# One load queue in order of need, an early ScalarE table load, and a new written-out order

## The chip, the cores and the metric

The kernel runs on one core of a Trainium2 chip. The core has five engines with a queue of instructions each: TensorE (PE, matmuls; its weight loads are listed as PEld), VectorE (DVE), ScalarE (ACT), GpSimd (POOL) and SyncE (SP, which here only issues transfers). Transfers run on the core's 16 DMA engines. They are issued from SP's or from ACT's queue, and an issue is an instruction of that queue like any other: what stands behind it waits for it. The metric is the device time of one execution in microseconds (us), as the median of several runs.

## What is computed

One transformer layer on x of 2048 tokens by 640 features, in bf16: linear attention with 32 heads of 20 features, and a feed-forward part with 1728 hidden features.

```python
def _A_ref(x, wqkv, w_phi, wo):
    qkv = (x @ wqkv).reshape(B, S, 3, H, Dh)           # q, k, v per head
    pq = einsum("bhsd,hdf->bhsf", q, w_phi)
    pk = einsum("bhsd,hdf->bhsf", k, w_phi)
    phi_q = concat([softmax(pq), softmax(-pq)], -1)
    phi_k = concat([softmax(pk), softmax(-pk)], -1)
    kv = einsum("bhsf,bhsd->bhfd", phi_k, v)
    z  = einsum("bhsf->bhf", phi_k)
    num = einsum("bhqf,bhfd->bhqd", phi_q, kv)
    den = einsum("bhqf,bhf->bhq", phi_q, z)[..., None] + 1e-6
    return (num / den) @ wo                            # heads joined again
def _B_ref(x, w1, w2):
    return silu(x @ w1) @ w2
h = x + _A_ref(layernorm(x), wqkv, w_phi, wo)
out = h + _B_ref(layernorm(h), w1, w2)
```

## The kernel before

The 2048 tokens are 16 tiles of 128, and 640 features are five chunks of 128. The whole program is a list of words, `ORDER`, read from left to right (lines 687 to 689). A word such as `kp.3` or `lx.1.2.a` calls `op_kp(3)` or `op_lx(1, 2, "a")`, and every engine's queue gets its instructions in the order of the words. Nothing is sorted later. So a word's place sets what it waits behind on its own engine. Semaphores between the engines are put in by the framework. A last letter names the engine or the queue: `a` is ACT, `v` DVE, `p` POOL, `s` SP. Ahead of the list stand eight filler matmuls (lines 685 and 686), and `wm` words add more; they multiply zeros and nobody reads them.

Stage 1 is the head. `lp` loads w_phi, `lk` chunks of the key weights into `wk`, `lv` those of the value weights into `wv`, `lx` tiles of x into `X`, `lo` the output weights. `wt.c` (line 301) transposes chunk c of `wk` with five matmuls, `wc.c` copies it from PSUM, `fk.c` (line 316) multiplies it with the block-diagonal w_phi that `ph` and `mk` build, and `fc.c` copies the result into `Wfk`, the key weights folded with w_phi. All five chunks are needed by every `kp`. `lq.c` loads a chunk of the query weights transposed, into `wk`'s space, once all `wt` have read it; `gk` and `gc` fold it in the same way.

Stage 2 does the keys and values. For tile t, `st` takes the statistics of the first layer norm on DVE, `rs` and `rm` finish them on POOL, `xn` normalises on DVE or ACT. Four tiles are transposed by PE (`xt`, copied by `xc`), twelve by a transposing transfer on SP (`xd`). `vp` and `kp` (line 344) are the two projections, ten matmuls each, `vc` copies the values, `ke` takes the two exponentials on ACT, `kr` sums and inverts them on DVE, `ka` scales them on POOL (`kb` half a tile on DVE), and `cc` (line 404) accumulates the key-value product, which `km` masks at the end of the stage.

Stage 3 does the queries and the attention's output. `qp.g.i` (line 424) projects the queries of four tiles for a part of the heads, and `qe` takes the exponentials. `dp` (line 458) is the product with the key-value matrix, `dw` and `dr` divide on DVE, `do` writes the two halves of a tile on DVE or POOL, `td` transposes it by a transfer, `op` (line 520) multiplies by the output weights, and `oa` adds the residual. `sq` (ACT), `sa` and `sr` (POOL) take the second layer norm's statistics, `hn` normalises and `hd` transposes it by a transfer.

Stage 4 is the feed-forward part, in groups of tiles (2, 4, 4, 4, 2): `up` (line 594 and 604), `ua` (Silu on ACT), `yp` and `yh` (line 640 and 655), `yo` adds the residual, `so` stores. `l1`, `l2` and `lh` load its weights. `ta` is a single exponential on one number, which makes ACT load the table that holds Exp. PSUM is four buffers of two banks, used by all products in turn.

Each transfer takes one of eight semaphores, in turn over both queues, so an issue waits for the eighth transfer before it.

Of the kernel before, what the change touches and what calls it, by code (L numbers as in the profile page):

```python
# [30 lines left out]
xn.4.v vp.0 ke.3 st.6 xd.4 xn.5.v kp.0 xc.1.a rs.6.2 st.8 lq.2 rm.6 st.11 kp.1 mc xn.6.a lq.1 xn.7.v
vc.0.a st.9 vp.1 xd.5 ke.0 st.15 kp.4 xd.6 vc.1.a st.10 ke.1 lq.4 gk.3 st.13 vp.4 rs.8.4 ke.4 xd.7
st.14 vp.5 rm.11 gc.3.a mo st.12 vc.4.a gk.1 kr.0 vc.5.a vp.6 rs.12.4 xn.11.a gc.1.a kp.7 xd.11 rm.8
rm.10 xn.13.v ka.0.p xn.10.a kr.1 kp.6 lq.0 vc.6.a ke.7 l1.2.s kr.4 kp.5 ka.1.p ke.6 kp.11 xn.8.a
xn.9.v xn.14.v xd.9 rm.15 kr.2 vp.7 rm.12 ke.11 ka.4.p xd.10 cc.1 vc.7.a kr.3 cc.0 ke.5 xd.13 vp.11
ka.2.p xn.12.a vp.9 kr.7 xn.15.a xd.12 ka.3.p kp.10 vc.9.a xd.8 kr.5 vc.11.a gk.4 ke.10 kp.13 xd.15
ka.7.p gc.4.a kr.10 xd.14 vp.10 kp.12 ka.5.p vc.10.a kr.6 cc.7 cc.2 ke.12 cc.4 ka.10.p cc.3 vp.14
ke.13 kr.12 kp.14 ka.6.p vc.14.a kr.13 gk.0 vp.13 gc.0.a ka.12.p kr.11 cc.10 vc.13.a cc.5 ke.14 kp.9
ka.13.p kp.8 ke.9 gk.2 kr.9 vp.8 ka.11.h gc.2.a kp.15 vc.8.a kr.14 ka.9.p qp.0.0 ke.15 ke.8 ka.14.p
qp.0.2 qe.0.0 kr.8 qp.0.1 qe.0.2 kr.15 ka.8.p vp.12 qe.0.1 kb.11 vp.15 ka.15.p vc.12.v cc.13 vc.15.v  # L40
# [6 lines left out]
dw.9.v sq.5 td.3 ua.0.3 sr.5 l2.8.13.s dp.6 do.4.0.v ua.0.1 up.0.2 dr.9 td.4 dw.6.v l2.0.4.s op.3
ua.0.2 dp.8 oa.3 op.10 dw.8.v sa.3 sq.3 sa.2 up.0.0 sr.3 dr.6 dr.8 do.6.1.p oa.10 op.4 ua.0.0 sr.2
hn.5 do.8.0.v do.8.1.p dp.7 oa.4 yp.1.1 td.8 hn.2 sa.4 sq.4 hn.3 do.9.1.p dw.7.v hd.3 sr.4 yp.1.0
hd.5 do.6.0.p do.9.0.v yh.0.0 td.6 hn.4 dp.11 yp.0.0 dw.11.v hd.2 yp.0.1 td.9 yo.1 hd.4 op.8 op.6  # L50
oa.8 dr.11 sa.8 yo.0 op.9 dr.7 so.0 oa.6 up.1.4 oa.9 sq.6 sa.9 sq.8 do.11.0.p up.1.0 ua.1.4 sa.6
sr.8 sa.10 dp.15 ua.1.0 up.1.1 dw.15.v sq.9 sr.9 up.1.3 ua.1.1 do.11.1.v sr.6 dr.15 do.15.1.v
do.7.0.p do.15.0.v do.7.1.v up.1.6 ua.1.3 hn.9 td.7 td.11 dp.13 ua.1.6 up.1.5 dw.13.v td.15 dp.12
ua.1.5 op.11 dw.12.v op.7 oa.11 up.1.2 oa.7 dr.13 dr.12 dp.14 ua.1.2 op.15 dw.14.v yp.2.0 oa.15 hn.6
yh.1.1 sa.15 sq.15 yh.1.0 dr.14 hd.6 do.12.0.v sa.11 yp.3.1 sq.10 do.13.0.v do.14.0.p sq.7 do.14.1.p
yp.2.1 sr.10 sa.7 hn.10 do.13.1.v sr.7 yp.4.1 yo.2 hn.8 sr.15 so.2 hn.7 td.13 do.12.1.v yp.5.0 hd.8
yp.3.0 td.14 op.13 hd.7 hd.9 yp.4.0 so.1 td.12 yp.5.1 yo.4 yo.3 so.4 hd.10 op.14 yo.5 up.2.3 oa.14
oa.13 sa.14 sa.13 up.2.1 up.2.2 up.2.5 ua.2.2 ua.2.3 ua.2.1 up.2.0 up.2.6 ua.2.0 sq.14 up.2.4 ua.2.6
ua.2.5 op.12 ua.2.4 sq.11 yp.7.1 oa.12 sr.11 sq.12 hn.11 yh.2.0 sq.13 yh.2.1 yp.9.1 sr.13 sr.14
yp.8.1 sa.12 hn.14 hn.15 sr.12 hd.14 yp.9.0 hn.12 hd.15 yp.8.0 yo.9 so.3 hd.11 yp.6.0 so.5 yo.8  # L60
hn.13 so.8 yp.6.1 so.9 hd.12 yp.7.0 yo.6 so.6 hd.13 up.4.2 yo.7 so.7 up.4.3 up.4.1 ua.4.3 ua.4.2
# [655 lines left out]
```

## Time and profile before

| | |
|---|---|
| median of 3 runs | 247.22 us (246.47 to 247.43) |
| the profiled execution | 246.91 us |
| its span | 244.9 us |
| PE busy | 235.9 us, 2148 matmuls |
| DVE, ACT, POOL busy | 135.2, 108.8, 87.3 us |
| mean granted clock | 0.993 |
| bytes moved | 20.60 MB |

The span runs from the first to the last recorded instruction. The profiled execution's own time has 2.0 us around it. Times in what follows are counted from the span's start. In a timeline's row, the first number is the start and the second the time from the first instruction's start to the last one's end; "xN" is the number of instructions, and the brackets give the idle time of the engine before them and what ended it. "ACTq" and "SPq" are the issuing of transfers in ACT's and SP's queue. The granted clock is a share of TensorE's full speed.

### The profile page before, as it was taken

Reading aid. Unit: us, or ns where it says so; the run is one execution under the profiler, and the core shown is the slowest. Engines: PE = TensorE matmul, PEld = TensorE weight load, DVE = VectorE, ACT = ScalarE, POOL = GpSimd, SP = SyncE. Lnnn points to the kernel's source line nnn. Section 1 sums busy time; section 2 is a strip of 40 time slices with the busy share of each in tenths; the row PEclk is TensorE's granted clock in tenths of the full one; section 3 lists DMA queues with packets and bytes.
Section 4 is the critical chain, followed back from the end, with each engine's and each line's share of the span. In section 5 each row is a group of like instructions: output and inputs, shape, how many; then the busy total and the mean of one; then the engine's idle time right before and its main releaser. Section 6 shows DMA issues by size and latency. Waiting matters only on the chain.

```text
span 244.9 us, 5196 instructions
## 1 busy us (share of the span) xinstructions
PE 235.9 (96%) x2148; PEld 152.2 (62%) x2162; DVE 135.2 (55%) x259; ACT 108.8 (44%) x158; POOL 87.3 (36%) x165
## 2 busy tenths in 40 slices
...
GB/s 191 357 306 66 133 60 198 102 12 0 3 3 0 29 195 173 182 173 116 121 95 3 54 29 27 60 117 95 0 3 28 174 97 0 0 3 0 0 87 76
DMA packets 42968, 20.60 MB, mean 84 GB/s; under 512 B 34368, under 2 KB 42560, under 8 KB 42944
## 3 DMA queue, kind: packets, MB, share of 16 engines
...
q8 instruction: 17, 0.28, 0.5%
q14 instruction: 7, 0.06, 0.1%
...
## 4 chain that ended last, share of the span: by engine, by line
PE 83%; DMA 6%; DVE 4%; SPq 2%; issue 2%; ACT 1%; POOL 1%; DVEq 0%; POOLq 0%
PE mm L594 23%; PE mm L640 20%; PE mm L344 18%; PE mm L520 6%; PE mm L424 5%; PE mm L404 3%; PE mm L458 2%; DMA HnT<-hn 2%; PE mm L316 2%; DMA X<-in_A_x_dram 2%; SPq L579 1%; DMA ot<-o 1%; PE mm L604 1%; DMA phr<-in_A_w_phi_dram 1%; DVE u L474 1%
## 5 line engine op out<-in xcount | busy, mean ns | idle before, releaser
L594 PE MATMUL mm<-HnT,w 128*128 128x512 bf16 (+1 forms) x317 | 58.0, 336 | 1.2 <-DMA HnT<-hn 0.7
L640 PE MATMUL mm<-w,shT 128*128 128x320 bf16 (+2 forms) x415 | 58.1, 299 | 0.1
L616 ACT ACTIVATE shT<-mm 128x1024 bf16<-128x1024 f32 (+2 forms) x29 | 27.0, 965 | 60.2 <-PE mm L594 43.9
L640 PEld LDWEIGHTS <-shT 128*128 128x128 bf16 x416 | 39.8, 98 | 17.3 <-issue 1.1
L594 PEld LDWEIGHTS <-w 128*128 128x128 bf16 x325 | 31.2, 98 | 24.7 <-DMA HnT<-hn 1.0
L663 DVE TENSOR_TENSOR ob<-mm,X 128x640 bf16<-128x640 f32 x15 | 12.1, 818 | 49.6 <-PE mm L640 42.5
L344 PEld LDWEIGHTS <-XnT 128*128 128x128 bf16 x320 | 30.7, 98 | 11.6
L382 POOL TENSOR_TENSOR Ek<-Ek,Sk 128x1280 bf16<-128x1280 bf16 (+1 forms) x16 | 36.7, 2322 | 2.3 <-DVE Sk L377 2.3
L374 DVE TENSOR_REDUCE Sk<-Ek 128x64 f32<-128x1280 bf16 x16 | 23.2, 1449 | 5.2 <-ACT Ek L366 5.2
L434 ACT ACTIVATE EqT<-mm 128x1024 bf16<-128x1024 f32 (+1 forms) x24 | 19.6, 888 | 10.9 <-PE mm L424 10.7
L520 PE MATMUL mm<-wo,ot 128*128 128x320 bf16 x160 | 23.9, 299 | 0.3 <-DMA ot<-o 0.2
L344 PE MATMUL mm<-wv,XnT 128*128 128x320 bf16 x160 | 23.9, 299 | 0.0
L344 PE MATMUL mm<-Wfk,XnT 128*128 128x320 bf16 x160 | 23.5, 299 | 0.0
L424 PE MATMUL mm<-XnT,Wfq 128*128 128x512 bf16 x95 | 22.8, 380 | 0.6 <-ACT EqT L434 0.3
L529 DVE SCALAR_TENSOR_TENSOR X<-mm,X 128x640 bf16<-128x640 f32 x16 | 12.8, 813 | 17.5 <-PE mm L520 17.5
L366 ACT ACTIVATE Ek<-mm 128x640 bf16<-128x640 f32 x32 | 20.5, 715 | 3.6 <-PE mm L344 2.3
L537 ACT ACTIVATE sq<-X 128x640 bf16<-128x640 bf16 x16 | 11.8, 735 | 21.4 <-DVE X L529 18.6
L520 PEld LDWEIGHTS <-ot 128*128 128x128 bf16 x160 | 15.2, 98 | 7.0 <-DMA ot<-o 0.5
L542 POOL TENSOR_SCALAR HM<-HST 128x1 f32<-128x1 f32 x16 | 3.7, 234 | 43.9 <-DVE X L529 43.9
L493 POOL TENSOR_TENSOR o<-u,rd 128x320 bf16<-128x320 f32 x18 | 13.1, 744 | 14.0 <-PE mm L424 9.7
L424 PEld LDWEIGHTS <-Wfq 128*128 128x128 bf16 x100 | 9.2, 98 | 11.0 <-issue 0.6
L474 DVE TENSOR_TENSOR u<-mm,w 128x672 f32<-128x672 f32 x16 | 13.7, 858 | 1.4 <-DVE w L472 0.3
...
## 6 DMA issues: line engine op xcount, KB each, us to landing
...
```

The costliest lines, as they stand in the source:

```text
L344: nc.tensor.matmul(ps[:, half, 0:320], tok(XnT[t // GT], t)[:, c, :], W[:, c, half * 320 : (half + 1) * 320], start=(c == 0), stop=(c == C ...
L366: nc.scalar.activation(Ek[:, s, :].rearrange("p (a n) -> p a n", a=2), tl["kp", t][:, :, 0:320], AF.Exp, scale=1.0 - 2.0 * s,)
L374: nc.vector.tensor_reduce(Sk[:], tl["ek", t][:].rearrange("p s (h f) -> p (s h) f", f=DH), axis=AX.X, op=ALU.add,)
L382: eng.tensor_tensor(Ek3, Ek3, tl["sk", t][:, lo:hi].unsqueeze(2).to_broadcast([P, hi - lo, DH]), op=ALU.mult,)
L424: nc.tensor.matmul(ps[:, k, :], Wfq[:, c, r * P : (r + 1) * P], XnT[g][:, c, :], start=(c == 0), stop=(c == C - 1),)
L434: nc.scalar.activation(E[:, s, rs[0] : rs[-1] + 1, :], tl["qp", g, i][:, 0 : len(rs), :], AF.Exp, scale=1.0 - 2.0 * s,)
L474: nc.vector.tensor_tensor(u[:], A[1][:, :, :, 0:21], w[:].unsqueeze(3).to_broadcast([P, 2, 16, 21]), op=ALU.mult,)
L493: (nc.vector if eng == "v" else nc.gpsimd).tensor_tensor(tl["o", t][:, a * 320 : (a + 1) * 320].rearrange("p (h f) -> p h f", f=DH), tl["u ...
L520: nc.tensor.matmul(ps[:, half, 0:320], tl["ot", t][:, c, :], wo[:, c, half * 320 : (half + 1) * 320], start=(c == 0), stop=(c == C - 1),)
L594: nc.tensor.matmul(ps[:, i * W : (i + 1) * W], w1[:, c, fc * P : (fc + 1) * P], HnT[g][:, c, 0:W], start=(c == 0), stop=(c == C - 1), skip ...
L616: nc.scalar.activation(sh[:, a:b], tl["up", g, k][:, 0 : b - a], AF.Silu)
L640: nc.tensor.matmul(ps, shT[g][:, fc * W + i * P : fc * W + (i + 1) * P], w2[:, fc, a:b], start=first and fc == 0, stop=last and fc == FC - ...
```

## The change

Only the list of words changes. At its head, all plain loads that stood on ACT's queue but w_phi's go to SP's (`lx.2.3.a` and `lx.3.4.s` become one `lx.2.4.s`, three `lv` become two), in another order: X 2:4, chunks 2, 0, 1 of `wk`, X 0, chunks 3 and 4, X 1, X 4:8, `wv`, and later X 8:12 and X 12:16. `lo` moves from the head to the middle. `ta` moves from near the end to ACT's second place. There are three `wm` words instead of six. The chunks are transposed in the order 2, 0, 1, 3, 4 instead of 1, 0, 4, 2, 3, and the folding follows; three `xt` stand ahead of the first projection, which is `kp.3` instead of `vp.2`.

After that the same operations come in another order throughout. Ten `xn` become fourteen on DVE, and ACT's six become two, with four `rm` less on POOL. Of the 32 halves of `do`, POOL gets 26 instead of 18. `l1`, `lh` and most `l2` words move from stage 3 into stage 2. `qp.1.2` comes before `km`, and `qp.3.2` and its `qe.3.2` come after the first group's `up` and `ua`.

```diff
 ORDER = """
-lp.a lk.1.2.s lx.2.3.a lk.0.1.s lk.4.5.a lk.3.4.s mk lk.2.3.a lx.3.4.s lx.0.1.a lv.0.2.s lv.2.4.a
-lv.4.5.s lx.1.2.a lx.4.8.s ph lo.s wt.1 st.2 wc.1.a wm.512 wm.512 wm.512 wt.0 lx.8.12.a rs.2 fk.1
-wc.0.v wt.4 fc.1.a wc.4.v wm.256 wt.2 fk.0 xn.2.v wc.2.a st.3 wm.512 xt.2 fc.0.a wt.3 fk.2 xc.2.a
-lq.3 wc.3.v fk.4 rs.3 fc.2.a wm.256 fk.3 vp.2 fc.4.a xn.3.v lx.12.16.s st.0 fc.3.a xt.3 st.1 kp.2
...
-cc.8 cc.11 cc.14 cc.9 cc.12 cc.6 cc.15 qp.1.0 km.1 close km.0 dp.1 qe.1.0 qp.1.1 dw.1.v dp.0 qe.1.1
-dr.1 qp.1.2 dw.0.v qe.1.2 qp.2.2 dr.0 do.1.1.v dp.2 qe.2.2 do.0.1.p qp.2.0 dw.2.v do.1.0.p do.0.0.p
-td.1 dp.5 td.0 qe.2.0 qp.2.1 dw.5.v lh.s l1.0.s dp.3 dr.2 qe.2.1 dr.5 op.1 dw.3.v do.5.1.p do.2.1.p
-op.0 do.5.0.p do.2.0.p oa.1 td.5 dp.10 oa.0 qp.3.2 td.2 dw.10.v sa.0 sq.0 qp.3.1 sa.1 l1.1.s sq.1
-sr.0 qe.3.2 sr.1 dr.10 hn.0 dp.4 qe.3.1 dr.3 hd.0 hn.1 qp.3.0 do.3.1.p dw.4.v hd.1 op.5 l2.4.8.s
-qe.3.0 dr.4 do.4.1.v op.2 oa.5 do.10.0.v sa.5 up.0.3 oa.2 do.10.1.p do.3.0.p dp.9 td.10 sq.2 up.0.1
...
-up.3.5 up.4.0 up.3.4 ua.4.0 ua.3.5 ta up.3.2 ua.4.1 up.3.6 ua.3.4 up.3.0 ua.3.6 ua.3.2 up.3.1 up.3.3
...
+lp.a lx.2.4.s ta lk.2.3.s lk.0.1.s mk lk.1.2.s lx.0.1.s lk.3.4.s lk.4.5.s lx.1.2.s st.3 lx.4.8.s
+wt.2 lv.3.5.s ph wt.0 lv.0.3.s wc.2.a wt.1 st.2 wc.0.a fk.2 wc.1.a st.0 wm.512 wt.3 rs.2.2 fc.2.a
+fk.1 wt.4 fc.1.a wc.3.v fk.0 rs.0 lq.1 wc.4.v wm.256 fk.3 fc.0.a xn.3.v fk.4 xn.2.v fc.3.a xt.3
+lx.8.12.s xn.0.v xt.2 fc.4.a xc.3.v lq.3 xt.0 st.6 wm.256 kp.3 xc.0.a xc.2.a lx.12.16.s st.7 lq.0
+kp.0 ke.3 st.1 rs.6.2 lq.4 kp.2 st.5 ke.0 rs.1 xn.6.v vp.3 st.4 ke.2 xd.6 xn.1.v rs.4.2 vp.2 st.11
+lq.2 vc.3.a mc st.9 xt.1 vp.0 xc.1.a st.10 vc.2.a gk.3 xn.5.v vc.0.a gk.0 xn.7.v vp.1 st.8 gc.0.a
+xd.7 xn.4.v rs.8.4 kp.1 kr.0 xd.5 vc.1.a gc.3.a gk.4 xd.4 vp.6 gc.4.a xn.10.v ka.0.p st.14 ke.1
+l1.1.s kp.6 lh.s st.13 vc.6.a st.15 kp.5 mo ke.6 st.12 gk.1 rm.8 gk.2 xn.9.v vp.4 rs.12.4 gc.2.a
...
+cc.11 cc.14 cc.13 cc.2 cc.10 vc.12.v cc.15 cc.8 cc.12 qp.1.0 km.1 close km.0 dp.1 qe.1.0 qp.1.1
+dw.1.v dp.0 qe.1.1 dr.1 qp.3.0 dw.0.v dp.3 qe.3.0 dr.0 qp.2.0 dw.3.v do.0.0.p do.0.1.p td.0 dp.5
+qe.2.0 dr.3 qp.2.1 do.3.1.v do.3.0.p dw.5.v do.1.1.p do.1.0.p op.0 td.1 qe.2.1 dr.5 do.5.1.p td.3
+dp.4 oa.0 do.5.0.p qp.2.2 dw.4.v sq.0 sa.0 td.5 op.1 sr.0 qe.2.2 hn.0 dp.2 dr.4 hd.0 op.3 oa.1
+do.4.0.p dw.2.v do.4.1.p sq.1 qp.3.1 sa.1 td.4 sr.1 hn.1 op.5 oa.3 qe.3.1 hd.1 dr.2 do.2.0.p op.4
+l2.0.4.s oa.5 do.2.1.v dp.10 td.2 up.0.2 dw.10.v up.0.3 oa.4 ua.0.2 dr.10 dp.9 ua.0.3 do.10.1.p sq.5
+up.0.1 dw.9.v sa.5 dp.6 ua.0.1 dr.9 up.0.0 dw.6.v do.9.1.p sq.3 sr.5 do.10.0.p op.2 hn.5 ua.0.0
+do.9.0.p dr.6 hd.5 sq.4 dp.8 oa.2 qp.3.2 td.10 dw.8.v sa.2 sq.2 yp.0.0 td.9 qe.3.2 sr.2 do.6.0.p
...
```

More of the change, by code (lines that the diff above doesn't have):

```diff
@@ L25 @@
 ORDER = """
-lp.a lk.1.2.s lx.2.3.a lk.0.1.s lk.4.5.a lk.3.4.s mk lk.2.3.a lx.3.4.s lx.0.1.a lv.0.2.s lv.2.4.a
-lv.4.5.s lx.1.2.a lx.4.8.s ph lo.s wt.1 st.2 wc.1.a wm.512 wm.512 wm.512 wt.0 lx.8.12.a rs.2 fk.1
-wc.0.v wt.4 fc.1.a wc.4.v wm.256 wt.2 fk.0 xn.2.v wc.2.a st.3 wm.512 xt.2 fc.0.a wt.3 fk.2 xc.2.a
-lq.3 wc.3.v fk.4 rs.3 fc.2.a wm.256 fk.3 vp.2 fc.4.a xn.3.v lx.12.16.s st.0 fc.3.a xt.3 st.1 kp.2
-rs.0 xc.3.a st.4 rs.1 vp.3 ke.2 xn.0.v st.5 xt.0 kp.3 xc.0.a xn.1.v rs.4.2 st.7 vc.2.a xt.1 vc.3.a
@@ L31 @@
[L31 to L40, printed above, removed]
@@ L46 @@
-qe.3.0 dr.4 do.4.1.v op.2 oa.5 do.10.0.v sa.5 up.0.3 oa.2 do.10.1.p do.3.0.p dp.9 td.10 sq.2 up.0.1
[L47 to L61, printed above, removed]
-up.3.5 up.4.0 up.3.4 ua.4.0 ua.3.5 ta up.3.2 ua.4.1 up.3.6 ua.3.4 up.3.0 ua.3.6 ua.3.2 up.3.1 up.3.3
-ua.3.1 ua.3.0 yp.15.1 ua.3.3 yh.4.0 yh.3.0 yp.12.1 yp.10.1 yp.15.0 yp.12.0 yo.15 yp.14.0 yp.14.1
@@ L64 @@
-yp.10.0 yo.14 yo.12 so.14 yh.3.1 yp.11.0 yo.10 so.10 yp.11.1 so.15 so.12 yq.13.0 yo.11 so.11 yq.13.1
-yz.13.0 yz.13.1 sz.13.0.a sz.13.1.s
+lp.a lx.2.4.s ta lk.2.3.s lk.0.1.s mk lk.1.2.s lx.0.1.s lk.3.4.s lk.4.5.s lx.1.2.s st.3 lx.4.8.s
+wt.2 lv.3.5.s ph wt.0 lv.0.3.s wc.2.a wt.1 st.2 wc.0.a fk.2 wc.1.a st.0 wm.512 wt.3 rs.2.2 fc.2.a
+fk.1 wt.4 fc.1.a wc.3.v fk.0 rs.0 lq.1 wc.4.v wm.256 fk.3 fc.0.a xn.3.v fk.4 xn.2.v fc.3.a xt.3
+lx.8.12.s xn.0.v xt.2 fc.4.a xc.3.v lq.3 xt.0 st.6 wm.256 kp.3 xc.0.a xc.2.a lx.12.16.s st.7 lq.0
@@ new lines @@
+kp.0 ke.3 st.1 rs.6.2 lq.4 kp.2 st.5 ke.0 rs.1 xn.6.v vp.3 st.4 ke.2 xd.6 xn.1.v rs.4.2 vp.2 st.11
+lq.2 vc.3.a mc st.9 xt.1 vp.0 xc.1.a st.10 vc.2.a gk.3 xn.5.v vc.0.a gk.0 xn.7.v vp.1 st.8 gc.0.a
+xd.7 xn.4.v rs.8.4 kp.1 kr.0 xd.5 vc.1.a gc.3.a gk.4 xd.4 vp.6 gc.4.a xn.10.v ka.0.p st.14 ke.1
+l1.1.s kp.6 lh.s st.13 vc.6.a st.15 kp.5 mo ke.6 st.12 gk.1 rm.8 gk.2 xn.9.v vp.4 rs.12.4 gc.2.a
+kr.6 xd.9 ke.5 vp.5 xd.10 xn.8.a xn.12.v ka.6.p xn.13.v kp.4 vc.5.a kr.3 xd.8 vc.4.a kp.7 ke.4 rm.11
+kr.5 ka.3.p vp.7 gc.1.a ke.7 qp.0.2 kr.4 xn.11.a kp.10 qe.0.2 xd.11 kr.7 ka.4.p vp.9 xd.12 kp.9
@@ new lines @@
+xn.14.v vc.9.a xn.15.v ka.7.p vc.7.a kr.2 xd.15 kp.11 l2.8.13.s xd.13 cc.4 ka.5.p cc.3 ke.10 cc.6
+l1.0.s cc.0 xd.14 cc.7 ke.9 kr.10 qp.0.0 l1.2.s ke.11 lo.s l2.4.8.s kr.9 ka.10.p kp.15 qe.0.0 kp.12
+kr.1 ke.15 ka.9.p qp.1.2 ke.12 kr.15 vp.8 ka.1.p vp.11 vc.8.a kr.11 qe.1.2 cc.5 ka.15.p cc.9 cc.1
+kr.12 kp.13 vc.11.a ka.11.p vp.10 ke.13 kp.14 vc.10.a kr.13 ka.12.h kp.8 ke.14 ka.2.p vp.14 ke.8
+kr.14 qp.0.1 vc.14.a kr.8 ka.14.p vp.13 kb.12 ka.13.p vp.15 vc.13.v vp.12 vc.15.a ka.8.p qe.0.1
+cc.11 cc.14 cc.13 cc.2 cc.10 vc.12.v cc.15 cc.8 cc.12 qp.1.0 km.1 close km.0 dp.1 qe.1.0 qp.1.1
@@ new lines @@
+do.9.0.p dr.6 hd.5 sq.4 dp.8 oa.2 qp.3.2 td.10 dw.8.v sa.2 sq.2 yp.0.0 td.9 qe.3.2 sr.2 do.6.0.p
+dr.8 yh.0.0 hn.2 sa.3 dp.7 yp.1.0 sr.3 dw.7.v do.6.1.p yp.1.1 sa.4 do.8.1.p do.8.0.v dr.7 sr.4 hn.3
+op.10 hd.3 yo.1 td.8 dp.11 oa.10 yp.0.1 dw.11.v sq.10 td.6 op.9 hd.2 hn.4 yo.0 op.8 hd.4 oa.9 op.6
+oa.8 sa.8 dp.13 oa.6 sa.9 up.1.5 dw.13.v sa.6 sq.6 do.7.0.p do.7.1.p up.1.1 ua.1.5 sr.6 td.7 dr.11
+dr.13 sq.8 do.11.1.p sq.9 do.11.0.p dp.15 up.1.2 td.11 dw.15.v sr.9 sr.8 up.1.3 sa.10 ua.1.2 ua.1.1
```

13 lines of the change are left out of this document (added).

## The prediction

> **What bounds the kernel now.** I read the page first, then PE's work and idle time by stage, then the timeline and the waits of the first 20 us, then the transfers.
>
> ```profile
> PE 235.9 (96%) x2148; PEld 152.2 (62%) x2162; DVE 135.2 (55%) x259; ACT 108.8 (44%) x158; POOL 87.3 (36%) x165
> PE 83%; DMA 6%; DVE 4%; SPq 2%; issue 2%; ACT 1%; POOL 1%; DVEq 0%; POOLq 0%
> ```
>
> TensorE is busy and carries the chain that ended last. Cut where the first projection begins (14.84 us, when its weights are loaded) and where the last matmul ends (241.86):
>
> ```profile
> 14.84:80.00 65.16, 64.96 (x777) 45.40 (x777) 54.91 (x94) 48.23 (x72) 47.53 (x51) 1.00 0.35 68
> 80.00:100.00 20.00, 19.46 (x188) 10.43 (x189) 18.43 (x39) 12.70 (x19) 8.41 (x19) 1.00 0.68 136
> 100.00:130.00 30.00, 29.10 (x304) 20.87 (x306) 22.07 (x49) 10.44 (x18) 11.98 (x34) 1.00 0.60 130
> 241.86:244.90 3.04, 0.00 (x0) 0.00 (x0) 0.29 (x1) 0.00 (x0) 0.00 (x0) 1.00 0.19 54
> sum 230.06, PE 224.94 PEld 145.26 DVE 129.09 ACT 103.27 POOL 83.79; mean PE 32.13 PEld 20.75 DVE 18.44 ACT 14.75 POOL 11.97
> ```
>
> The first number after the stretch is its length, the second PE's busy time. Over 227.02 us PE works 224.94 us and idles 2.1. A new order of the same work can save there at most these 2.1. The sum: 14.84 head + 224.94 work + 2.1 idle + 3.04 tail = 244.9, the span; the profiled execution took 246.91, 2.0 more. So the head is the place to win. In it:
>
> ```profile
> 7.22 0.33 ACTq L219 DMA_DIRECT2D X<-in_A_x_dram  x1
> 7.58 1.28 ACT L161 ACT_TABLE_LOAD   x1 [7.58 <-DMA X<-in_A_x_dram]
> 8.88 0.69 ACT L161 COPY wTk<-mm 128x640 bf16<-128x640 bf16 x1
> 9.62 0.49 PE L316 MATMUL mm<-phb,wTk 128*128 128x140 bf16 x6 [2.49 <-ACT wTk L161]
> 9.95 0.44 PE L301 MATMUL mm<-ident,wk 128*128 128x128 bf16 x5
> 14.89 1.52 PE L344 MATMUL mm<-wv,XnT 128*128 128x320 bf16 x10
> ```
>
> ScalarE stands in `lx.1.2.a`, an issue that must wait for an earlier transfer's semaphore, until 7.22, then loads its table, and only then copies the chunk whose transpose ended at 5.4. PE's queue is in order, so `fk.1` and all behind it wait 2.49 us, though the last piece of `wk` landed at 7.7 (issued 2.3, 5.4 to landing).
>
> ```profile
> 7.00:8.00 1.00, 0.13 (x2) 0.00 (x0) 0.49 (x1) 0.42 (x1) 0.00 (x0) 1.00 1.02 375
> 8.00:9.00 1.00, 0.00 (x0) 0.00 (x0) 0.00 (x0) 0.99 (x2) 0.00 (x0) 1.00 0.98 356
> 11.00:12.00 1.00, 1.00 (x8) 0.60 (x6) 1.00 (x3) 0.91 (x2) 0.00 (x0) 0.50 1.01 396
> 12.00:13.00 1.00, 0.94 (x10) 0.86 (x9) 0.28 (x2) 0.52 (x2) 0.52 (x2) 0.50 0.98 371
> ```
>
> The last three numbers are the granted clock, the DMA share and GB/s: the gap is paid twice, since quarter-microsecond windows show the clock at half from 10.35 to 13.76. DMA is full from 2 to 15 us.
>
> **The change, part by part.** *Landings.* All loads stand on one queue. From before's windows the bytes moved by 3, 4, ... 12 us are 0.25, 0.57, 0.80, 1.13, 1.46, 1.84, 2.19, 2.53, 2.88, 3.27 MB; a landing follows its last byte by about 0.8 (X 12:16: last bytes about 19.3, landed 20.1). In the new order X 2:4 lands at 3.9, `wk` 2, 0, 1 at 4.6, 5.2, 5.8, X 0 at 6.4, `wk` 3, 4 at 6.9, 7.3, X 1 at 7.8, X 4:8 at 9.6, `wv` at 10.6 and 12.0. Seven issues of 0.33 to 0.55 leave ACT; on SP eight of 0.43 end at 4.1, ahead of the bytes. The ninth transfer on must wait for the eighth before it, but over 1 MB is queued then: no gap. The last `wk` piece gains only 0.4 us.
>
> *ScalarE.* One issue (0.46), then the table, 1.28: ready at 2.6 instead of 8.86.
>
> *The head's chain*, with before's durations: transposes of a chunk 0.54 at half clock, 0.28 at full; `fk` 0.6 and 0.3; ACT copies 0.65; DVE statistics 1.1, mask product 1.0, copy 0.5, normalisation 0.42. The first eight fillers run at half clock (0.43 apart; the 128x512 matmul takes 0.22 later), and I take full clock from 6.9, one window of 3.41 (13.76 less 10.35) before 10.35: fillers were still 0.43 apart at 6.0, and `wt.4` at 10.1 took 0.28.
> PE: `wt.2` 4.63 to 5.17, `wt.0` to 5.75, `wt.1` to 6.35, `fk.2` to 6.9, filler, `wt.3` to 7.5, `fk.1`, `wt.4`, `fk.0` to 8.4.
> ACT: `wc.2`, `wc.0`, `wc.1` 5.3 to 7.2; `fc.2` to 7.9, `fc.1` to 8.6, `fc.0` to 9.25.
> DVE: `st.3` from 3.9, `ph` to 6.05, `st.2`, `st.0` to 8.2, `wc.3`, `wc.4` to 9.2, `xn.3`, `xn.2`, `xn.0` to 10.45, `xc.3` to 10.95.
> So `fk.3` 8.8 to 9.1, `fk.4` 9.3 to 9.6, `fc.4` 9.85 to 10.5, `xt.3`, `xt.2`, `xt.0` by 10.8, and `kp.3`, the first projection, at 11.1: DVE sets it. Two more transposes (0.56) are then done than at 14.84 before. Gain 14.84 - 11.1 + 0.56 = 4.3 us.
>
> *Fillers.* Before issues six after the first eight, after three; all fit in waits, so 0. Without that cover (PE never waiting) they would cost 0.4 at full clock.
>
> *What follows the first projection.* PE has 12 us of work up to `vp.6` (8 projections of 1.36, three `gk` of 0.32, a transpose), due at 23.2. `vp.3` (15.2) needs `wv` (12.0). `vp.6` needs `xd.6`, behind 4.9 MB on SP. At 0.35 MB/us for loads and 0.18 for the transposes among them (0.194 at 16 to 17) its bytes end near 19.6, landed by 20.6: slack 2.6. Its `xn.6` is ready at 15.7. `wo` (800 KB) no longer stands among the loads.
>
> *The normalising chain.* DVE and POOL must come forward with PE. DVE takes four `xn` of 0.41 from ACT (0.95 each), +1.6; POOL sheds four `rm` of 0.33. `kr.0` starts at about 22.4 (29.93 before), the last `kr` (2.0 each) ends near 61, the last `ka` (2.2 each) at 63, and its `cc` is due at about 69 (the last `cc` ends at 11.1 + 58.4 - 0.56 + 1.13 = 70.1, the 58.4 from 14.84 to 73.24 before). Before, the last `ka` ended at 72.15, some 0.6 ahead of its `cc`. So no new wait: 0.
>
> *To the first `up`.* After the last `cc`, PE had 25.9 us of work up to `up.0.3` and idled about 1.5; now it has 25.0 (`qp.1.2` has gone ahead, `qp.3.2` behind, one `op` comes in). Replaying the DVE chain (`dw` 2.4, `dr` 0.35, `oa` 0.85, `hn` 0.45) and the two halves of `do` on POOL (0.74 each), `hd.1` lands 25.9 after the last `cc`: about 1.1 idle, where before paid 1.5. Before's `hd.1` took 5.4 to land among w1 and w2 loads (2.6 where none run); those loads now go into 24 to 50 us. Eight more `do` halves lie on POOL (6.0 there, 3.4 less on DVE). At best all idle here goes (-1.1); at worst two tokens of the chain pay a second POOL half of 0.74 each (+1.5). I take 0 against before, as POOL is only 12 of 30 us busy at 100 to 130.
>
> *Table loads in the middle.* `qe.3.2` (Exp) now stands behind the first `ua` (Silu), so the compiled order has three loads there instead of one, and none at the end, where `ta` had two:
>
> ```profile
> 208.77 1.28 ACT L249 ACT_TABLE_LOAD   x1
> 210.27 1.28 ACT L616 ACT_TABLE_LOAD   x1
> ```
>
> PE lost 0.05 around those. In the middle ACT is busy 10.4 of 30 us; 2 x 1.28 hide, at worst 2.6 where `sq`, and so `hn`, stands behind them. I take 0, nearest to the row at 208.77. The Trainium skill's page "ScalarE: Activation LUTs" (What ACT_TABLE_LOAD costs) speaks against the move: it adds a drain of about 1.38 to each switch, 2.66 in all, so up to 5.3 here. Here the copy behind the load of 7.58 starts at 8.88, 1.30 after it, and so no drain shows.
>
> Sum: 11.1 + (224.94 - 0.56) + 2.1 + 3.04 = 240.6, and 2.0 around it: 242.6 against 246.91. The median shown (247.22) is 0.3 above the profiled run, so **242.9** as a median, 1.7% faster. A difference under 0.5% (1.2 us) is what a measurement of this kernel can't tell from none.
>
> **Rivals.** *The clock stays or goes low* (0.16). With fewer fillers the window up to 6.9 holds more transposes (1.6 us of 3.4, against 1.0). If the gate then opens only at 10.3, the head's chain becomes PE's: +0.7, 243.6. If the gaps between 6.9 and 10.3 (PE about 73% busy; 27% closed it before, 97% opened it) close it up to 13.8, the projections lose half of 3.41: +1.7, 244.6. The Trainium skill's "TensorE: Matmul & The Clock Gate" (Part 4: PE-mode transpose) says that transposes do not count as busy in the same way; by that the first of these times holds. The trace does not decide: the window before 6.9 opened the gate with 30% transposes.
>
> *The middle gets a new wait* (0.13): the switches and POOL's extra halves delay `sq`, `sr`, `hn`, and up.1 waits as up.0 did. Price 1.3 to 4: 244 to 247, say 245.5. For it: the only PE waits after 14 us lie at `up` and `op` behind such chains (0.7 and 0.2). Against: up.1 has a slack of about 1.7 by the same replay.
>
> *Slower* (0.12, of which 0.10 over the bound): one queue is too slow. `vp.6` waits for `xd.6`, which stands behind every load and four weight transposes, 5.1 MB in all. It gets as late as before's time plus 0.5% if it lands at 28.8 instead of 23.2 (a loss of 4.3 + 1.2), that is at a mean below 0.20 MB/us. For it: windows with transposes moved 194 to 213 GB/s (15 to 17 us). Against: SP's queue alone moved 371 and 355 GB/s at 96 to 97 and 100 to 101 us. At 0.19 the time is about 249.5.
>
> *The reordering buys nothing*: `wk` lands hardly sooner, so this part can be empty, and ACT's freedom alone still brings nearly all, since DVE's list sets 11.1. It is inside the forecast. *More* (0.04): no idle at `up.0` and a head of 10.3, 241.0 or less.
>
> **How the numbers follow.** Forecast 0.55 (241.0 to 243.9). 241.0 to 246.0 holds it, the clock and two thirds of the middle rival: 0.80. Faster by over 0.5% (below 246.0): 0.55 + 0.16 + 0.09 + 0.04 = 0.84; within: 0.06; slower: 0.10.
>
> **What would show it.** ACT's table load before 3 us and no wait of PE for `wTk` over 0.6; first projection at 10.3 to 12, `kp.3` behind DVE's `xc.3`; granted clock 1.00 from 7 us on, or half windows for the rival; PE idle from there to the last matmul about 2.1; `vp.6` without a wait at 23; `up.0.2` near 96.2 (100.66 before); table loads near 95 to 115. I am wrong if PE idles more than 3 us after the first projection, or that comes later than 12.5.

## The result, and the profile after

The changed kernel takes 243.74 us (median of four runs, 243.62 to 244.17), the kernel before 246.84 in the same comparison. The ratio is 0.9877 (0.9847 to 0.9907): 1.2% or 3.1 us faster, where 242.9 us and 1.7% were forecast. The profiled execution took 243.84 us with a span of 241.7, against 246.91 and 244.9. In a later comparison, together with the last four kernels below, the changed kernel came out at 0.9932 (0.9903 to 0.9961), so its gain is 2 to 3 us.

The page of the changed kernel, engines and then the chain that ended last:

```profile
PE 233.3 (97%) x2143; PEld 150.3 (62%) x2159; DVE 137.0 (57%) x255; ACT 105.8 (44%) x154; POOL 89.8 (37%) x167
...
PE 74%; DVE 15%; DMA 4%; POOL 3%; ACT 1%; issue 1%; POOLq 0%; ACTq 0%
```

TensorE is as busy as before, but it carries 74% of the chain instead of 83%, and DVE 15% instead of 4%. That is the first sign that something besides PE now sets a stretch. The head first, in the timeline of all engines and, for the last two rows, of PE:

```profile
1.28 1.28 ACT L249 ACT_TABLE_LOAD   x1 [1.28 <-PEq L701]
...
4.70 1.37 PE L301 MATMUL mm<-ident,wk 128*128 128x128 bf16 x15
...
5.19 1.88 ACT L161 COPY wTk<-mm 128x640 bf16<-128x640 bf16 x3 [2.41 <-PE mm L301]
...
10.29 4.24 PE L344 MATMUL mm<-Wfk,XnT 128*128 128x320 bf16 x30
14.37 2.88 PE L344 MATMUL mm<-wv,XnT 128*128 128x320 bf16 x20
```

ACT has its table at 2.6 us and copies the first chunk at 5.19 (8.88 before); the first projection starts at 10.29 (14.89). With the two transposes (0.56) that are now done ahead of it, the head gives 14.89 - 10.29 + 0.56 = 5.2 us. From there to the last matmul's end the kernel before took 241.86 - 14.89 = 227.0 us, 226.4 without those transposes. The changed one takes 238.7 - 10.29 = 228.4, so 2.0 are lost behind the head, and 5.2 - 2.0 = 3.2 is the whole difference of the spans. PE's waits behind the head say where:

```profile
PE mm L404 <- POOL Ek L382: 2.0, 3, 0.9
PE mm L316 <- DMA wk<-in_A_wqkv_dram: 0.8, 1, 0.8
PE mm L458 <- ACT EqT L434: 0.2, 1, 0.2
```

(The numbers are us in total, how often, and the longest.) `cc` waits three times, 2.0 us in all, for POOL's scaling `ka`, and `gk.0` waits 0.8 for a chunk of the query weights. These 2.8 are new. Some 0.8 of idle time elsewhere has gone, the stall at the first `up` above all, which leaves the 2.0. The same waits in PE's timeline:

```profile
19.99 0.23 PE L316 MATMUL mm<-phb,wk 128*128 128x140 bf16 x1 [0.76 <-DMA wk<-in_A_wqkv_dram]
...
41.95 1.72 PE L404 MATMUL mm<-Vp,Ek 128*64 128x84 bf16 x80 [0.43 <-POOL Ek L382]
44.35 0.57 PE L404 MATMUL mm<-Vp,Ek 128*64 128x84 bf16 x20 [0.68 <-POOL Ek L382]
...
55.60 0.57 PE L404 MATMUL mm<-Vp,Ek 128*64 128x84 bf16 x20 [0.90 <-POOL Ek L382]
```

POOL is not simply too slow: it stands and waits for DVE's sums, 1.9 us at a time (second and last row of the second fence below). So the question is what DVE does. DVE's timeline, then POOL's:

```profile
22.23 1.48 DVE L374 TENSOR_REDUCE Sk<-Ek 128x64 f32<-128x1280 bf16 x1
...
24.48 0.88 DVE L259 BATCH_NORM_STATS2 stats<-X 128x6 f32<-128x320 bf16 x2
...
28.50 0.39 DVE L276 TENSOR_SCALAR xn<-X,MV,RS 128x640 bf16<-128x640 bf16 x1
...
30.79 2.77 DVE L276 TENSOR_SCALAR xn<-X,MV,RS 128x640 bf16<-128x640 bf16 x2
33.48 1.47 DVE L374 TENSOR_REDUCE Sk<-Ek 128x64 f32<-128x1280 bf16 x1
...
41.25 3.23 DVE L276 TENSOR_SCALAR xn<-X,MV,RS 128x640 bf16<-128x640 bf16 x2
44.40 1.47 DVE L374 TENSOR_REDUCE Sk<-Ek 128x64 f32<-128x1280 bf16 x1
```

```profile
31.02 2.36 POOL L382 TENSOR_TENSOR Ek<-Ek,Sk 128x1280 bf16<-128x1280 bf16 x1 [0.91 <-ACT xn L281]
...
35.62 2.36 POOL L382 TENSOR_TENSOR Ek<-Ek,Sk 128x1280 bf16<-128x1280 bf16 x1 [1.88 <-DVE Sk L377]
39.55 7.15 POOL L382 TENSOR_TENSOR Ek<-Ek,Sk 128x1280 bf16<-128x1280 bf16 x3 [1.57 <-ACT Vp L161]
48.57 15.15 POOL L382 TENSOR_TENSOR Ek<-Ek,Sk 128x1280 bf16<-128x1280 bf16 x7 [1.87 <-DVE Sk L377]
```

A normalisation `xn` takes 0.39 us at 28.50, but two of them take 2.77 at 30.79 and 3.23 at 41.25, where POOL scales a tile. An `xn` that starts while a scaling runs ends 0.2 us after that scaling; one that starts before it is not held (0.35 us for the one at 30.79). All durations of `xn` on DVE, shortest, median and longest in ns, in the kernel before and in the changed one:

```profile
L276 DVE TENSOR_SCALAR xn<-X,MV,RS x10: 380/416/1271, 10.8 to 37.3; 128x640 bf16<-128x640 bf16 x10
```

```profile
L276 DVE TENSOR_SCALAR xn<-X,MV,RS x14: 347/418/2505, 8.6 to 42.0; 128x640 bf16<-128x640 bf16 x14
```

The four late ones should take 4 x 0.41 = 1.6 us and take 6.0, so 4.4 us of DVE are lost, and the sums (1.45) and all that stands behind them in DVE's queue come so much later. The sums themselves and the statistics run beside POOL at their usual durations. The row of before already held one such case, 1.271, which the median of 0.416 hid. The Trainium skill's page "SBUF — State Buffer" (SBUF: two separate sides) states a rule that fits: DVE, for some of its instructions, and GpSimd share a pair of ports, which the instruction that starts first holds for its whole length while the other engine is blocked. For `xn` against the scaling the trace agrees, 2.5 us in place of 0.39. That the ports are the reason is not shown here.

### The profile page after: what moved, and what is told of

Its sections match the earlier page's. It is cut to its first block, busy times and chain, and to the rows that moved or that the text cites. A ratio compares the mean times of both kernels' runs of the same rounds, so it can differ in the third digit from the quotient of the medians.

```text
span 241.7 us, 5181 instructions
## 1 busy us (share of the span) xinstructions
PE 233.3 (97%) x2143; PEld 150.3 (62%) x2159; DVE 137.0 (57%) x255; ACT 105.8 (44%) x154; POOL 89.8 (37%) x167
## 4 chain that ended last, share of the span: by engine, by line
PE 74%; DVE 15%; DMA 4%; POOL 3%; ACT 1%; issue 1%; POOLq 0%; ACTq 0%
PE mm L594 24%; PE mm L640 23%; PE mm L520 9%; PE mm L424 7%; PE mm L344 5%; DVE Sk L374 5%; DMA X<-in_A_x_dram 4%; DVE stats L259 4%; DVE xn L276 3%; PE mm L458 3%; POOL Ek L382 3%; PE mm L404 2%; DVE Sk L377 1%; PE mm L604 1%; PE mm L655 1%
## 5 line engine op out<-in xcount | busy, mean ns | idle before, releaser
L382 POOL TENSOR_TENSOR Ek<-Ek,Sk 128x1280 bf16<-128x1280 bf16 (+1 forms) x16 | 36.9, 2332 | 7.5 <-DVE Sk L377 5.0
L493 POOL TENSOR_TENSOR o<-u,rd 128x320 bf16<-128x320 f32 x26 | 19.2, 753 | 23.9 <-DVE rd L487 14.1
L434 ACT ACTIVATE EqT<-mm 128x1024 bf16<-128x1024 f32 (+1 forms) x24 | 19.9, 880 | 10.7 <-PE mm L424 10.6
L537 ACT ACTIVATE sq<-X 128x640 bf16<-128x640 bf16 x16 | 11.7, 734 | 16.6 <-DVE X L529 16.1
L259 DVE BATCH_NORM_STATS2 stats<-X 128x6 f32<-128x320 bf16 x32 | 13.7, 469 | 4.0 <-DMA X<-in_A_x_dram 3.8
```

What stands on the lines that cost most here:

```text
L259: nc.vector.bn_stats(stats[:, k, :], X[:, t, k * 320 : (k + 1) * 320])
L382: eng.tensor_tensor(Ek3, Ek3, tl["sk", t][:, lo:hi].unsqueeze(2).to_broadcast([P, hi - lo, DH]), op=ALU.mult,)
L434: nc.scalar.activation(E[:, s, rs[0] : rs[-1] + 1, :], tl["qp", g, i][:, 0 : len(rs), :], AF.Exp, scale=1.0 - 2.0 * s,)
L493: (nc.vector if eng == "v" else nc.gpsimd).tensor_tensor(tl["o", t][:, a * 320 : (a + 1) * 320].rearrange("p (h f) -> p h f", f=DH), tl["u ...
```

## The experiments

Each time of the kernel before is from the same chip and hour: 246.49 us for the first four kernels, 246.5 for the next four, 246.4 for the last four. Single executions of one kernel lay up to 2.5 us from its median there, so waits and starts in the profile weigh more than a few tenths of a median. The changed kernel itself was run beside the last four only. The others are held against its two ratios, 0.9877 and 0.9932, so a gain of less than about 1 us would not show in them.

**The table load alone.** The kernel before, with `ta` as second word and the late one gone:

```diff
-lp.a lk.1.2.s lx.2.3.a ... ua.3.5 ta up.3.2
+lp.a ta lk.1.2.s lx.2.3.a ... ua.3.5 up.3.2
```

> The kernel before with one word moved: the early table load (ta) in ACT's second place, gone from its late place. Theory (ACT's late table load and its blocked issues hold up the head): the copy of the first wk chunk still waits for the issue that ends at 7.55, but no longer for the 1.28 of the table, so it starts at 7.6 instead of 8.88, PE's idle gap shrinks from 2.5 to about 1.2, the first projection comes about 1.3 earlier (13.5), time about 245.6. Rival (the landings set the head): first projection stays within 0.4 of 14.84 and the time within 0.5 of before.

Measured: 245.3 us, ratio 0.9959 (0.993 to 0.9988). ACT's first copy and the work behind it, in the timelines of ACT and PE:

```profile
7.71 0.69 ACT L161 COPY wTk<-mm 128x640 bf16<-128x640 bf16 x1 [4.93 <-DMA X<-in_A_x_dram]
```

```profile
8.46 0.49 PE L316 MATMUL mm<-phb,wTk 128*128 128x140 bf16 x6 [2.80 <-ACT wTk L161]
...
12.00 1.52 PE L344 MATMUL mm<-wv,XnT 128*128 128x320 bf16 x10
```

The copy starts 1.2 us sooner, as the load's 1.28 says. It still stands behind the issue that waits for an earlier transfer and ends at 7.7. PE waits 2.80 for it, where 1.2 was expected and the kernel before shows 2.49: PE came to this point sooner in this execution. The first projection is 2.9 earlier in this profile; the further 1.7 goes with the clock, which showed no half windows here (its price is measured below). The median is 1.2 lower, but the load alone does not account for that: 7 of these 10 executions had a mean clock of 0.998 or more, against 6 of 27 of the kernel before. (One window of 3.41 us at half clock in 245 us makes 0.993.) Among executions with such a full clock the medians are 244.8 and 245.1, among the others 245.9 and 246.7.

**The loads alone.** The kernel before, with only its early loads on SP in order of need:

```diff
-lp.a lk.1.2.s lx.2.3.a lk.0.1.s lk.4.5.a lk.3.4.s mk lk.2.3.a lx.3.4.s lx.0.1.a lv.0.2.s lv.2.4.a
-lv.4.5.s lx.1.2.a lx.4.8.s ph lo.s ... lx.8.12.a
+lp.a lx.2.4.s lk.1.2.s lk.0.1.s mk lk.4.5.s lx.0.1.s lk.2.3.s lk.3.4.s lx.1.2.s lx.4.8.s lv.3.5.s
+ph lv.0.3.s lx.8.12.s lo.s ...
```

> The kernel before with only its early loads changed: all but w_phi on SP in the order in which the old list needs them (chunks of wk 1, 0, 4, 2, 3), X 8:12 ahead of wo. ACT then has no blocking issue, so its table load comes at 1.3 by itself. Theory: the first wk copy starts near 5.4 instead of 8.88 and PE has no gap over 0.7, but the old list's first projection is a value projection that needs wv, which lands at about 13.5 on one queue as in the changed kernel: first projection near 13.6, time about 245.5. Rival (freeing ACT is all there is): first projection near 11, time about 243. Rival (one queue is worse): wv later than 14.8, time 247 or more.

Measured: 247.31 us, ratio 1.004 (1.001 to 1.0071), so slower. PE's timeline:

```profile
6.12 0.49 PE L316 MATMUL mm<-phb,wTk 128*128 128x140 bf16 x6
...
9.41 0.49 PE L316 MATMUL mm<-phb,wTk 128*128 128x140 bf16 x6
13.53 0.71 PE L344 MATMUL mm<-wv,XnT 128*128 128x320 bf16 x2 [3.63 <-DMA wv<-in_A_wqkv_dram]
```

With no waiting issue ahead, ACT's table load goes first by itself and the folding ends at 9.9. But this list begins with a value projection, whose weights are now last: PE waits 3.63 us, and the projections then run at half clock. The first projection came where it was expected (13.6), the time did not (245.5). With this list the loads do not pay; what they give with `kp.3` as the first projection was not run by itself.

**The half clock.** The kernel before, with fillers in the gap behind `wt.0`, first eight `wm.512` words:

```diff
-wm.512 wt.0 lx.8.12.a rs.2 fk.1
+wm.512 wt.0 wm.512 wm.512 wm.512 wm.512 wm.512 wm.512 wm.512 wm.512 lx.8.12.a rs.2 fk.1
```

> The kernel before with eight more filler matmuls ahead of its first wait for ScalarE, nothing else. Theory (the halved clock from 10.35 to 13.76 is a cost of its own of the old head): the fillers fill the gap of 2.5 (1.8 at full clock), the gate stays open, the first projection comes 1.0 to 1.6 earlier at the same loads and table load, and the slower ones among the kernel's executions go: median 245.3 to 245.8. Rival (the old head waits for ACT and the loads whatever the clock): no gain, 246.5, or up to 0.9 slower where the fillers still run at half clock.

Measured: 248.0 us, ratio 1.0068 (1.0035 to 1.0101), which says nothing on the clock, for the gap stayed:

```profile
9.74 1.46 PE L254 MATMUL mm<-warm 128*128 128x512 bf16 x6 [3.12 <-ACT wTk L162]
```

Each filler takes a PSUM buffer in turn. The third found it held by the chunk that ACT had not copied, and six fillers then ran ahead of `fk.1` (1.46 us). So again, with nine fillers that share one buffer:

```diff
+    def op_wf(k):
+        ps = mm2()
+        for i in range(k):
+            op_wm(512, ps)
...
-wm.512 wt.0 lx.8.12.a rs.2 fk.1
+wm.512 wt.0 wf.9 lx.8.12.a rs.2 fk.1
```

> The kernel before with nine filler matmuls behind wt.0, all into one PSUM buffer, so that none of them can wait for ScalarE's copy (in the run with eight separate ones the third waited 3.1 for it, and six then ran behind the wait, ahead of the real work). Theory (the gap of the old head shuts the clock gate in a part of the executions, and that is a cost of its own): the gap is filled, no half clock after 7 us, the first projection never later than 14.2, the slow part of the executions (246.4 to 247.8) goes: median 245.0 to 245.8 against 246.5. Rival (the clock is hidden behind ACT and the loads): no difference, 246.5 within 0.4.

Measured: 245.51 us, ratio 0.9973 (0.9948 to 0.9998).

```profile
6.77 2.11 PE L253 MATMUL mm<-warm 128*128 128x512 bf16 x9
9.31 0.49 PE L321 MATMUL mm<-phb,wTk 128*128 128x140 bf16 x6 [0.43 <-ACT wTk L161]
...
12.86 1.39 PE L349 MATMUL mm<-wv,XnT 128*128 128x320 bf16 x9
```

`fk.1` starts hardly sooner (9.31 against 9.62), yet the first projection comes at 12.86 instead of 14.89, with no half window. In the medians this is 0.9 us, with an interval that almost reaches no gain. So the gap was paid twice, as the prediction read it, but not in every execution. All 12 of this run had a mean clock of 0.998 or more, and 21 of the 77 of the kernel before in the three comparisons. Those 21 have a median of 244.9 us, the other 56 one of 246.7, so half windows go with 1.8 us there. All 15 executions of the changed kernel had the full clock. Its medians (243.74 and 244.34) are 0.6 to 1.2 us below those 21, so more than half of its gain goes with the half windows being gone.

**The head's last microsecond.** The changed kernel with four of its loads back on ACT's queue, behind the table:

```diff
-lp.a lx.2.4.s ta lk.2.3.s lk.0.1.s mk lk.1.2.s lx.0.1.s lk.3.4.s lk.4.5.s lx.1.2.s st.3
+lp.a ta lx.2.4.a lk.2.3.s lk.0.1.s mk lk.1.2.s lx.0.1.a lk.3.4.s lk.4.5.a lx.1.2.a st.3
```

> The changed kernel with four of its early loads (X 2:4, X 0, wk chunk 4, X 1) back on ACT's queue, behind the table load; same words otherwise. Theory (the single queue is worth little, the table load and the list are worth the head): first projection between 10.0 and 11.0 as with one queue, time within 0.5 of 243.7. Rival (one queue in order of need carries the gain): pieces from two queues land interleaved, chunk 3 or 4 or X 0 a microsecond later, first projection at 11.5 or later, 1 us slower or more.

Measured: 244.26 us, ratio 0.9931 (0.9894 to 0.9967), level with the changed kernel's 0.9932 of the later comparison. PE's timeline and its waits:

```profile
11.66 4.24 PE L344 MATMUL mm<-Wfk,XnT 128*128 128x320 bf16 x30
```

```profile
PE mm L404 <- POOL Ek L382: 1.6, 2, 0.9
```

The first projection is 1.4 us later than in the changed kernel, but the span of the profiled execution is the same, 241.7. The wait of `gk.0` is gone, `cc` waits 0.4 less, and the second stretch of `cc` begins at 41.85 instead of 41.95. So what the head gains below 11.7 us is lost again in stage 2, which DVE and POOL set by then: DVE takes the statistics of X 4:8 from 11.41 here, and from 11.27 in the changed kernel, where it had stood 1.14 us for that load. As expected the time stays within 0.5 us, although the first projection comes as late as the rival had it. Three of these 12 executions had half windows (245.1 to 246.8), none of the changed kernel's 15; beyond that no gain of the single queue shows.

**The new waits, one at a time.** Three edits of the changed kernel. First the transposing load for `gk.0` earlier:

```diff
-lx.12.16.s st.7 lq.0 kp.0
+lq.0 lx.12.16.s st.7 kp.0
```

> The changed kernel with the transposing load of query chunk 0 ahead of the load of X 12:16. The wait of gk.0 for it (0.76) should go. Theory (stage 2 is set by DVE and POOL, not by PE's queue): the cc matmuls then wait as much longer for POOL, and the time stays within 0.4 of the changed kernel's 243.7. Rival (PE's own waits add up): 0.7 faster, 243.0.

Measured: 243.97 us, ratio 0.9911 (0.9881 to 0.9942). The wait of `gk.0` is gone and `cc` waits more:

```profile
PE mm L404 <- POOL Ek L382: 2.9, 3, 1.3
```

PE arrived sooner at the same late scalings. Then the four late `xn` in one group, so that they meet one running scaling less:

```diff
-xn.13.v kp.4 ... xd.12 kp.9 xn.14.v vc.9.a xn.15.v ka.7.p
+xn.13.v xn.14.v xn.15.v kp.4 ... xd.12 kp.9 vc.9.a ka.7.p
```

> The changed kernel with two words moved: the normalisations of tiles 14 and 15 stand right behind that of tile 13, the same instructions on the same engines. Theory (DVE's normalisations stand still while POOL scales a tile, and this makes POOL and the cc matmuls late): the four wait once, behind the scaling of tile 6, instead of twice, the 3.2 us at 41.3 go, the sums behind them come 2.4 earlier, PE's waits for POOL's Ek fall from 2.0 to under 0.7, time 1.3 to 2 below the changed kernel (about 242). Rival (DVE merely has too much work in this stage): the same amount of work, so the waits stay at about 2.0 and the time within 0.4 of 243.7.

Measured: 243.95 us, ratio 0.9909 (0.9875 to 0.9942). DVE's timeline and PE's waits:

```profile
31.07 3.48 DVE L275 TENSOR_SCALAR xn<-X,MV,RS 128x640 bf16<-128x640 bf16 x4
```

```profile
PE mm L403 <- POOL Ek L381: 1.8, 2, 1.2
```

The four take 3.48 us instead of 6.0, and the third `cc` wait is gone. But the sums behind them come 0.7 later, and the first two `cc` waits grow from 1.1 to 1.8. The gain of 1.3 to 2 that was expected did not come. Third, on top of the earlier load, PE's order to suit the order in which POOL finishes (`cc.4`, `cc.7` and `cc.1` later):

```diff
-cc.4 ka.5.p cc.3 ke.10 cc.6 l1.0.s cc.0 xd.14 cc.7 ke.9 kr.10 qp.0.0 ... cc.9 cc.1 kr.12 kp.13
+cc.0 cc.6 cc.3 qp.0.0 cc.4 cc.7 ka.5.p ke.10 l1.0.s xd.14 ke.9 kr.10 ... cc.9 kr.12 kp.13 cc.1
```

> The changed kernel with only TensorE's waits served: five cc of stage 2 in the order 0, 6, 3, then qp.0.0, then 4 and 7; cc.1 behind kp.13; the transposing load of query chunk 0 ahead of X 12:16. No instruction of DVE or POOL moves. Theory (DVE and POOL set the end of stage 2): the waits at 41, 44 and 55 go, but POOL's last scaling still ends near 71.4 and the last eight cc wait for it instead, 1.5 to 2.5 us; time within 0.5 of the changed kernel (243.7). Rival (PE's waits add up and POOL has slack): PE waits for POOL under 0.5 in all, about 2.5 faster, 241.3.

Measured: 243.93 us, ratio 0.9896 (0.9863 to 0.9929).

```profile
PE mm L344 <- DMA XnT<-xn: 1.3, 1, 1.3
PE mm L424 <- ACT Ek L366: 0.7, 1, 0.7
PE mm L344 <- DVE Vp L159: 0.4, 1, 0.4
```

No `cc` waits, but `kp.15` now waits 1.3 for its transposed tile, since `xn.15` stood still beside POOL until 44.8. So a late `xn` sets this wait.

**The standstill avoided, and shortened.** Two ways, both on top of that order and of the earlier load. The four late `xn` on ACT:

```diff
-xn.12.v ... xn.13.v ... xn.14.v ... xn.15.v
+rm.12 rm.13 rm.14 rm.15 ... xn.12.a ... xn.13.a ... xn.14.a ... xn.15.a
```

> The same, and the normalisations of tiles 12 to 15 on ACT (0.95 each) instead of DVE, with the four small POOL instructions that this form needs. Theory (the stall of DVE's normalisations beside POOL's scaling makes the chain late): DVE no longer stops at 31 and 41, the sums come 3 to 5 us earlier, POOL's last scaling ends by 69, PE waits for POOL under 0.5, and the time is 1.5 to 2.5 below the changed kernel: 241.2 to 242.2. Rival (POOL's own 36.9 us of scaling are the limit): last scaling still after 71, no gain over the run with TensorE's order alone.

Measured: 243.85 us, ratio 0.9905 (0.9872 to 0.9939).

```profile
PE mm L344 <- ACT Vp L161: 1.4, 1, 1.4
PE mm L424 <- ACT Ek L366: 0.7, 1, 0.7
```

DVE no longer stands still beside POOL: its sums follow each other from 28.9 to 40.1. But ACT is late instead: a projection waits 1.4 us for a buffer that ACT has to copy out, DVE waits 3.6 for ACT's exponentials, and nothing is won. Neither theory had that. And the earlier edits together, the four `xn` in one group and the new order of PE (with the earlier load for `gk.0`, not shown again):

```diff
-xn.13.v kp.4 ... xn.14.v vc.9.a xn.15.v ka.7.p
+xn.13.v xn.14.v xn.15.v kp.4 ... vc.9.a ka.7.p
...
-cc.4 ka.5.p cc.3 ke.10 cc.6 l1.0.s cc.0 xd.14 cc.7 ke.9 kr.10 qp.0.0 ... cc.9 cc.1 kr.12 kp.13
+cc.0 cc.6 cc.3 qp.0.0 cc.4 cc.7 ka.5.p ke.10 l1.0.s xd.14 ke.9 kr.10 ... cc.9 kr.12 kp.13 cc.1
```

> The changed kernel with TensorE's order of the run before last (cc 0, 6, 3, qp.0.0, cc 4, 7; cc.1 behind kp.13; query chunk 0's load earlier) and the normalisations of tiles 14 and 15 right behind that of 13. Theory (the stall of DVE beside POOL's scaling ended the saving of TensorE's order alone, by the transpose of tile 15): the wait for XnT (1.3) goes, the waits for cc stay away, and what is left is POOL's last scaling near 71.4: about 1.0 under the changed kernel on the same chip. Rival (whatever is served in the middle is lost at the end of stage 2): as the changed kernel within 0.4, with a wait of over 1 for POOL in the last cc.

Measured: 242.37 us (242.21 to 243.2), ratio 0.9868 (0.9834 to 0.9902). As its control ran the changed kernel once more, as it is:

> The changed kernel itself, on the same chip as the others of this call, to compare them with: 243.7 within 0.5, PE waiting about 2.0 for POOL's Ek and 0.8 for the query weights.

Measured: 244.34 us (243.26 to 245.07), ratio 0.9932 (0.9903 to 0.9961), with the same waits for `cc` (2.0). So the edits together give 2.0 us, and all 6 executions lie below all 11 of the control, where none alone showed a gain. PE's waits and POOL's scalings with them:

```profile
PE mm L423 <- ACT Ek L365: 0.7, 1, 0.7
PE mm L593 <- DMA HnT<-hn: 0.3, 1, 0.3
```

```profile
40.24 29.68 POOL L381 TENSOR_TENSOR Ek<-Ek,Sk 128x1280 bf16<-128x1280 bf16 x13 [1.57 <-DVE Sk L376]
```

No `cc` and no projection waits. POOL scales 13 tiles in a row without a pause and ends at 69.9 (71.7 in the changed kernel), and the last `cc` ends at 70.9 (73.1 in the control, whose head was the same within 0.1 us). This version is faster than both kernels. A last one asked whether POOL's row of 13 is now the limit, with half of one scaling on DVE:

```diff
-ka.8.p
+ka.8.h ... kb.8
```

> The same, and half of the scaling of tile 8, POOL's last one, on DVE (1.36 there, 1.15 less on POOL). Theory (POOL's last scaling ends stage 2): the last cc come about 1 us earlier, 0.5 to 1.0 under the run without this and 1.5 to 2 under the changed kernel, 241.8 to 242.4. Rival (TensorE itself or something else ends stage 2): no further gain.

Measured: 242.48 us, ratio 0.9869 (0.9834 to 0.9904), no gain over 242.37. POOL's row is 0.6 us shorter (29.11), but a new wait stands where DVE now copies later:

```profile
PE mm L343 <- DVE Vp L158: 0.4, 1, 0.4
```

So whether POOL's row limits this version stays open.

## Why the prediction was right and wrong

The direction was right, and 243.74 lies in its range, inside the likeliest case's own (241.0 to 243.9). The point was 0.8 us low. The profiled execution missed its own sum by more, 243.84 against 242.6, in this way: the head 0.9 better, the idle time behind it 2.0 worse (2.8 of new waits less 0.8 saved), 0.1 from what lies around the span. That the first two have opposite signs is luck: the head hid almost half of the idle time.

- *Landings*: right where it counted. The `wk` pieces let their transposes start at 4.70, 5.14 and 5.61 (landings of 4.6, 5.2, 5.8 forecast). The later ones were 1.5 us late (X 4:8 at 11.2 instead of 9.6, `wv` at 12.1 and 13.5 instead of 10.6 and 12.0), but `vp.3` starts at 14.37 and PE waited for none of them. DVE did, for X 4:8, where the prediction had no wait:

```profile
11.27 0.89 DVE L259 BATCH_NORM_STATS2 stats<-X 128x6 f32<-128x320 bf16 x2 [1.14 <-DMA X<-in_A_x_dram]
```

- *ScalarE*: right, ready at 2.6. The first experiment lowers the median by 1.2 us with the table load alone, in part by fewer half windows, and the second shows that freeing the queue without the new first projection loses.
- *The head's chain*: 10.29 against 11.1, and 10.4 to 11.0 in other runs of this head. By the durations (fillers 0.43 apart, then 0.28 for a chunk's transposes) the full clock was there from about 4.7 us in this execution, where 6.9 was assumed. In other profiled executions it came between 4.3 and 6.9, so this part was luck. That `xc.3` on DVE would set `kp.3` was right: that copy starts at 9.64 and ends 0.1 before the projection's first weights.
- *The normalising chain, "So no new wait: 0"*: this is the step that failed. It cost the moved `xn` at "four `xn` of 0.41", +1.6 us of DVE, from durations of `xn` that had run alone. With the tiles come forward, four stand beside POOL's scalings and take 6.0. The first `kr` came on time, at 22.2. From 24.45, POOL's scalings are 36.9 us of work and would have ended at 61.4 in a row. But POOL stands without one for 10.3 us: 4.2 before the second, while DVE has the statistics of four tiles and two `xn` in its queue, 2.2 and 1.9 behind the two meetings of `xn` and scaling, 2.0 elsewhere. So the last `ka` ended at 71.7, not 63, only 1.0 before the last `cc`'s end, and `cc` paid 2.0 us. Two more things were left out. The forecast's 38.6 us from the first `kr` to the end of the last are before's 38.7, but before had no statistics left by then and three `xn`, where the changed list has four tiles' statistics (24.48 to 28.58) and six `xn`; it took 43.6. And only the last `cc` was held against POOL, while the waits fell on the 4th, 5th and 9th scaling.
- *What follows the first projection*: `vp.6` did not wait, as forecast, but "three `gk` of 0.32" were counted as work without asking when `lq.0` lands, behind X 12:16 and beside other transposes on SP: 0.8 us. It was no loss by itself, as its removal only moved the wait to `cc`.
- *To the first `up`*: no wait at all, where 1.1 was forecast. `up.0` starts at 97.88, later than the forecast of 96.2 only because the last `cc` ends 2.5 later. This gave back most of the 0.8.
- *Table loads in the middle*: three, as read from the compiled order. PE waited 0.2 behind one of them:

```profile
109.93 1.28 ACT L434 ACT_TABLE_LOAD   x1
111.22 1.08 ACT L434 ACTIVATE EqT<-mm 128x512 bf16<-128x512 f32 x2
...
112.36 0.37 PE L458 MATMUL mm<-KVBD,EqT 64*128 64x88 bf16 x10 [0.22 <-ACT EqT L434]
```

The activation starts 1.29 us after its load starts, and the instruction ahead of the load ends at 109.91, so no drain shows behind it or before it. The rule of the Trainium skill's "ScalarE: Activation LUTs" (What ACT_TABLE_LOAD costs) that was weighed, a drain with each load, did not hold here.

- *The clock rival*: it did not come. The clock was full from 4.7 us to the end, so the 243.6 and 244.6 are out. Whether transposes count for the clock stays open. From 4.70 to 8.11 PE was busy 3.26 of 3.41 us, 2.23 of it with transposes, and the clock stayed full: 96% with them, 30% without. The window that closed it before (6.94 to 10.35) had 27% with them and 10% without, so both ways of counting fit. "TensorE: Matmul & The Clock Gate" (Part 4: PE-mode transpose) of the Trainium skill says that transposes do not count as busy in the same way; no run here decides it.
- *The middle's rival* had the right size of trouble in the wrong place: the second layer norm was in time, and the first one's DVE and POOL were not. *The slow queue* did not come.

That PE would idle more than 3 us behind the first projection was named as a sign of being wrong. The profile shows 4.0 there, 2.0 more than forecast, and a better head hid 0.9 of it.

What stays open: how much of the 2.0 us comes from the standstill of `xn` and how much from the statistics behind the first `kr` was not separated. The gain of grouping the `xn` and reordering PE was taken together, and the collision of the first pair (3.48 us for four) is still in the fastest version. The version without any collision moved the work to ACT, which then was late, so what a free DVE alone would bring was not seen.
